# A two-layer expert behind a chunked mLSTM: the 64-row tail of w_in as pairs of 64-row products, the gates' weights summed in PSUM, and another order of work

## The chip, the cores and the metric

The kernel runs on one core of a Trainium2 chip. The time is device microseconds of one execution; before the change the median of three runs is 478.81 us (476.74 to 479.77). All times below are in microseconds unless a unit is given.

## The reference

Attention part, for every batch and head (B, H, S, D = 4, 8, 768, 40), step by step over S:

```python
m_new = np.maximum(f_gate[:, :, t] + m, i_gate[:, :, t])
f_stab = np.exp(f_gate[:, :, t] + m - m_new)
i_stab = np.exp(i_gate[:, :, t] - m_new)
C = f_stab[:, :, None, None] * C + i_stab[:, :, None, None] * np.einsum('bhd,bhe->bhde', vt, kt)
n = f_stab[:, :, None] * n + i_stab[:, :, None] * kt
h_tilde = np.einsum('bhde,bhe->bhd', C, qt)
denom = np.maximum(np.abs(np.einsum('bhd,bhd->bh', n, qt)[:, :, None]), 1.0)
y[:, :, t] = (1.0 / (1.0 + np.exp(-o_gate[:, :, t]))) * h_tilde / denom
```

Its y, heads side by side, is x [3072, 320]. Then the expert layer, in float32:

```python
h = x @ w_in                           # [320, 2048]
relu6 = np.clip(h + 3.0, 0.0, 6.0)
return ((h * relu6 / 6.0) @ w_out)     # [2048, 320]
```

## The kernel before, in words

**Tiling.** The 3072 tokens are eight units of 384 (three chunks of 128). For each unit the attention is made in two tasks of heads, chunk by chunk, and then x of this unit goes through the expert layer. Unit u+1's attention is made between the products of unit u.

**Gates** (`gates(c0, n)`, L415 to L504). The gates of all 32 (batch, head) rows are handled along the free axis, in four calls of 1, 1, 1 and 3 chunks (`GP`). On DVE: a scan gives the running maximum m (L439), two passes make the log forget factor (L445, L447), a second scan its running sum (L449), two subtractions the exponent of the input weight (L442, L460). PE then turns the results (L468, L469, L472) into the PSUM tile `pc`, DVE copies them out (L474, L477, L481), PE spreads each chunk's last column with the constant `last` (L495), DVE adds (L497), and ACT takes the exponentials wT, dec and eG (L483, L499, L501).

**Attention products** (`group`, L647). The tiles `xy` get batches of 16 small fp32 products each, 64 rows by 64 columns of the array: L669, L676, L685, L690. `fin` (L756) normalises, transposes to xa (L791) and splits x into xh (cast, L795) and xl (rest, L797).

**Expert weights.** w_in and w_out come as 64-bit words; `weight_slice` (L806) makes float32 of them in eight slices each, then splits w_in into fp32r parts: whi and wlo hold 256 of the 320 rows (as two tiles of 128 rows), and wtl the last 64 rows, high part in one half of the partitions and low part in the other. The tail's two casts (on ACT) and subtractions (L851, L852) are instructions of 64x128. `split_out` (L858) splits w_out into vh and vl.

**Expert products.** `mm1(u, f)` (L883) makes h of one feature block f (128 of 2048 features) for 384 tokens from eight products of 128 rows, 128 columns and 384 tokens (L895): six over the 256 rows, and two with wtl, which carry the tail's high and low weights in one product. `g = h * clip(h + 3, 0, 6) / 6` is an activation on ACT (L909) and a product with h on DVE (L911); then g is split into gh (L385) and gl (L919). `mm2(u, p)` (L924) multiplies two feature blocks with w_out: for each of three token tiles six products of 320 columns (L938 to L940). Unit 0 uses plain float32 there (L936). h has two PSUM buffers (`mm=2` in the plan's slots).

**Order.** All engines' instructions are put out in an order that a planner (`Plan`) works out when the kernel is built: every piece of work is a generator with a due time (worked out from constants such as T0, SPAN, AH and G0, plus an offset for its number from the table OFS), and the planner simulates the engines with fixed costs and takes what is ready and due first. `ENGINES` is a string of 30 letters: for each kind of elementwise work, which engines may do it. The scheduler then keeps this order. Until the expert layer opens (`open_moe`), PE is given filler products (`warm`, L403).

Of the kernel before, what the change touches and what calls it, by code (L numbers as in the profile page):

```python
# [49 lines left out]
T0H = -19.089  # L50
SP0 = 7.143
LST = 0.974
LVP = 0.547
LGW = 0.628
SPAN = 50.902
T0 = 57.141
AH = 8.377
GP = [1, 1, 1, 3]
G0 = 3.567
G1 = 5.981  # L60
AH1 = 33.544
# [65 lines left out]
class Plan:  # L127
# [119 lines left out]
    def run(self):  # L247
        self.settle()
        while self.jobs:
            best = {}  # L250
            for j in self.jobs:
# [14 lines left out]
                if j["hot"]:  # L266
                    start = max(self.free[e], 0.0)
                    if self.heat(start):
# [3 lines left out]
                        continue  # L272
                k = (late, start if late else 0.0, j["due"] + (j["req"][2] if len(j["req"]) > 2 and e != "q" else 0.0), j["n"])
# [55 lines left out]
def mlstm_moe_kernel(ctx: ExitStack, tc: tile.TileContext, ig, fg, qkd, natd, ond, w_in, w_out, ident_d, out):  # L329
# [31 lines left out]
    plan = Plan(dict(wm=1, xy=1, exy=1, z=1, es=1, eo=1, st=2, nat=2, gw=NGW, ht=2, on=1, x=2,  # L361
# [31 lines left out]
    def warm():  # L393
# [12 lines left out]
        f_s=[BR, S], i_s=[BR, S], m_s=[BR, S], lf=[BR, S], g_s=[BR, S], last=[128, 128], gTs=[128, NC, BH], cTs=[128, NC, BH], one=[BR, S // 2 + L], sel=[BR, 4, Q]).items()}  # L406
# [8 lines left out]
    def gates(c0, n):  # L415
        f_s, i_s, m_s, lf, g_s, last, gTs, cTs, one, sel = (GT[k] for k in ("f_s", "i_s", "m_s", "lf", "g_s", "last", "gTs", "cTs", "one", "sel"))
        if c0 == 0:
# [5 lines left out]
            nc.vector.memset(lf[:, 0:1], 0.0)  # L423
# [13 lines left out]
        hs = slice(c0, c0 + n)  # L437
        yield "d", ld(w)
        nc.vector.tensor_tensor_scan(m_s[:, a:z], f_s[:, a:z], i_s[:, a:z], m_s[:, a - 1 : a] if c0 else NEG, ALU.add, ALU.max)  # L439
        b, t = max(a, 1), plan.now["t"]  # L440
        e = yield psub(26, w)
        E(e).tensor_sub(i_s[:, a:z], i_s[:, a:z], m_s[:, a:z])  # L442
        ti, plan.now["t"] = plan.now["t"], t
        yield "d", ld(w)
        nc.vector.tensor_add(lf[:, b:z], f_s[:, b:z], m_s[:, b - 1 : z - 1])  # L445
        yield "d", ld(w)
        nc.vector.tensor_sub(lf[:, b:z], lf[:, b:z], m_s[:, b:z])  # L447
        yield "d", ld(2 * w)
        nc.vector.tensor_tensor_scan(g_s[:, a:z], one[:, :w], lf[:, a:z], 0.0, ALU.mult, ALU.add)  # L449
# [3 lines left out]
        t = plan.now["t"]  # L453
# [4 lines left out]
        plan.now["t"] = max(t, ti)  # L458
        yield "d", ld(w)
        nc.vector.tensor_sub(i_s[:, a:z], i_s[:, a:z], g_s[:, a:z])  # L460
        for c in cs:
            event(f"i_s{c}")
        yield "wait", "ident"
        gs = yield "get", "es"
        pc = bank(gs, [128, 3, n, BH], f"pc{c0}")
        yield "p", mat(6 * n, 64, 1, 32, 32)
        for c in cs:
            nc.tensor.transpose(pc[:, 0, c - c0, :], g_s[:BH, c * L : (c + 1) * L], ident[:BH, :BH])  # L468
            nc.tensor.transpose(pc[:, 1, c - c0, :], i_s[:BH, c * L : (c + 1) * L], ident[:BH, :BH])  # L469
        for s in range(2 * n):  # L470
            for h in range(2):
                nc.tensor.matmul(pc[h * Q : h * Q + Q, 2].rearrange("p n (c r) -> p (n c) r", c=2)[:, s], i_s[:BH, a + s * Q : a + s * Q + Q], ident[:BH, 16 * h : 16 * h + 16], start=True, stop=True)  # L472
        yield "d", cd(32 * n)
        nc.vector.tensor_copy(gTs[:, hs], pc[:, 0])  # L474
# [6 lines left out]
        nc.vector.tensor_copy(cTs[:, hs], pc[:, 1])  # L481
# [7 lines left out]
        go = yield "get", "eo"
        pl = bank(go, [128, 2, n, BH], f"pl{c0}")  # L490
        yield "p", mat(2, 32 * n, 2)
        nc.tensor.matmul(pl[:, 0], last, gTs[:, hs], start=True, stop=True)
        for c in range(2):
            for h in range(2):
                nc.tensor.matmul(pl[h * Q : h * Q + Q, 1].rearrange("p n (c r) -> p n c r", c=2)[:, :, c], last[:, c * Q : c * Q + Q], gTs[:, hs, 16 * h : 16 * h + 16], start=True, stop=True)  # L495
        yield "d", cd(32 * n)
        nc.vector.tensor_tensor(wT[:, hs], pl[:, 0], cTs[:, hs], ALU.add)  # L497
# [601 lines left out]
```

## Time and profile before

| | before |
|---|---|
| median of 3 runs | 478.81 us (476.74 to 479.77) |
| the profiled execution | 479.48 us, span 477.8 us |
| mean granted TensorE clock | 0.981 of full speed |
| instructions that count as work: PE, DVE, ACT, POOL | 5741, 811, 330, 259 |
| packets and bytes of DMA | 21245 packets, 47.66 MB |

The profile is that of one execution. "Busy" is the time in which an engine has an instruction of its own running; PE is TensorE's products, PEld its weight loads, which run beside them. A row of a group reads: line, engine, operation, output and inputs by their names, shapes, how often, then busy time and mean ns of one, then idle time of the engine just before and what ended it. A row of the timeline reads: start, duration, engine, line, operation, names, and in brackets the idle time before it. Products are pipelined: the next one starts before the last one's duration is over, so what a product costs is read from start to start. A window row reads: stretch, its length, busy time and instructions of PE, PEld, DVE, ACT and POOL, granted clock, share of the DMA engines' time, GB/s.

The page's list of groups also names idle time: POOL idles 158.1 us ahead of L919, 130.1 of them for gh, and ACT 186.1 us ahead of L909 for h.

### The profile page before, as it was taken

The page shows a single profiled execution, that of the slowest core. Times are in us where ns is not written, and L with a number is a line of the kernel's source. Part 1 is how long each engine was busy: PE and PEld are TensorE (multiplying, and loading weights), DVE is VectorE, ACT ScalarE, POOL GpSimd, SP SyncE. Part 2 cuts the span into 40 slices and gives each one's busy share as a digit, 9 for nine tenths or more (in the row PEclk, how much of TensorE's full clock was granted, in tenths as well). Part 3 has the DMA queues.
Part 4 walks back from the last instruction along what each step waited for, and adds up shares of the span by engine and source line. Part 5 has one row for each costly group of instructions (what it writes and reads, how often), then busy time and mean ns, then how long its engine had stood idle before and what let it go on. Part 6 is the DMA issues. An engine that isn't in the chain of part 4 may idle for free.

```text
span 477.8 us, 13585 instructions
## 1 busy us (share of the span) xinstructions
PE 464.4 (97%) x5741; PEld 435.8 (91%) x5741; DVE 307.4 (64%) x811; ACT 168.6 (35%) x330; POOL 185.9 (39%) x259
## 2 busy tenths in 40 slices
PE   8999889899999999999999999999999999999997
PEld 7898777777999999999999999999999999999996
DVE  5569799899878857576657466738554646334332
ACT  1234778895322422232324122322322221222112
POOL 3324331112565444445444353435453333333432
PEclk8599999999999999999999999999999999999999
DMA  7356678871152541435142151516041010001001
GB/s 238 96 163 232 173 253 242 240 269 49 43 150 57 137 140 53 115 79 150 45 122 70 50 143 37 115 44 177 16 117 43 2 43 3 1 1 42 1 1 41
DMA packets 21245, 47.66 MB, mean 100 GB/s; under 512 B 2360, under 2 KB 15416, under 8 KB 21184
## 3 DMA queue, kind: packets, MB, share of 16 engines
q1 hardware_dynamic: 21184, 46.79, 33.5%
q8 instruction: 45, 0.74, 0.7%
q14 instruction: 16, 0.13, 0.1%
HBM read 42.75 MB, written 4.03 MB: 98 GB/s over the span
## 4 chain that ended last, share of the span: by engine, by line
PE 86%; DVE 4%; ACT 4%; DMA 3%; issue 2%; SPq 0%; ACTq 0%; DVEq 0%
PE h L895 34%; PE acc L938 11%; PE acc L940 10%; PE acc L939 10%; PE pw L403 5%; PE xy L685 3%; PE xy L669 2%; PE xy L690 2%; PE acc L936 2%; PE xy L676 2%; PE xa L791 2%; DMA rawo<-in_w_out_dram 1%; DMA gw<-gsc 1%; ACT g L909 1%; DMA i_s<-in_ig_dram 1%
## 5 line engine op out<-in xcount | busy, mean ns | idle before, releaser
L919 POOL TENSOR_TENSOR gl<-g,gh 128x384 fp32r<-128x384 f32 x112 | 119.7, 1069 | 158.1 <-DVE gh L385 130.1
L911 DVE SCALAR_TENSOR_TENSOR g<-g,h 128x384 f32<-128x384 f32 x128 | 70.6, 552 | 128.3 <-ACT g L909 127.5
L909 ACT ACTIVATE g<-h,half 128x384 f32<-128x384 f32 x128 | 74.1, 579 | 204.8 <-PE h L895 186.1
L938 PE MATMUL acc<-vh,gh 128*128 128x320 f32 x336 | 104.3, 310 | 0.0
L940 PE MATMUL acc<-vh,gl 128*128 128x320 f32 x336 | 103.8, 309 | 0.0
L939 PE MATMUL acc<-vl,gh 128*128 128x320 f32 x336 | 103.5, 308 | 0.0
L895 PE MATMUL h<-xh,whi 128*128 128x384 f32 x256 | 93.7, 366 | 0.5 <-DVE g L911 0.5
L895 PE MATMUL h<-xl,whi 128*128 128x384 f32 x256 | 85.9, 336 | 0.0
L895 PE MATMUL h<-xh,wlo 128*128 128x384 f32 x256 | 85.9, 335 | 0.0
L938 PEld LDWEIGHTS acc<-vh,gh 128*128 128x128 f32 x336 | 63.0, 188 | 0.3
L940 PEld LDWEIGHTS acc<-vh,gl 128*128 128x128 f32 x336 | 63.0, 187 | 0.3 <-POOL gl L919 0.3
L939 PEld LDWEIGHTS acc<-vl,gh 128*128 128x128 f32 x336 | 63.0, 188 | 0.0
L729 POOL TENSOR_TENSOR C<-C,dec 128x84 f32<-128x84 f32 x77 | 30.8, 400 | 79.7 <-DVE C L731 56.2
L895 PEld LDWEIGHTS h<-xh,whi 128*128 128x128 f32 x256 | 48.1, 188 | 4.6 <-DVE g L911 2.0
L895 PEld LDWEIGHTS h<-xl,whi 128*128 128x128 f32 x256 | 48.3, 188 | 0.7
L895 PEld LDWEIGHTS h<-xh,wlo 128*128 128x128 f32 x256 | 48.1, 188 | 0.0
L385 DVE CAST gh<-g 128x384 fp32r<-128x384 f32 x112 | 42.1, 375 | 2.6
L895 PE MATMUL h<-xl,wtl 128*128 128x384 f32 x128 | 43.3, 338 | 0.0
L895 PE MATMUL h<-xh,wtl 128*128 128x384 f32 x128 | 43.0, 336 | 0.0
L573 POOL TENSOR_TENSOR nat<-nat,wT 128x168 f32<-128x168 f32 x48 | 27.6, 592 | 24.3 <-DMA nat<-in_nat_dram 17.5
L403 PE MATMUL pw<-ones 128*128 128x128 bf16 x397 | 30.9, 241 | 2.1 <-POOL ones L397 1.1
L936 PE MATMUL acc<-vr,g 128*128 128x320 f32 x96 | 28.0, 437 | 3.2 <-DVE vr L836 3.2
(107 smaller groups left out, 650.1 us busy)
## 6 DMA issues: line engine op xcount, KB each, us to landing
st<-in_qk_dram SPq DMA_DIRECT2D x28, 300.0 KB
nat<-in_nat_dram SPq DMA_DIRECT2D x16, 492.0 KB
gw<-gsc SPq DMA_DIRECT2D x28, 192.0 KB
rawi<-in_w_in_dram SPq DMA_DIRECT2D x8, 640.0 KB
rawo<-in_w_out_dram SPq DMA_DIRECT2D x8, 640.0 KB
nat<-in_nat_dram SPq DMA_DIRECT2D x16, 252.0 KB
on<-in_on_dram SPq DMA_DIRECT2D x8, 480.0 KB
out_dram<-ob SPq DMA_DIRECT2D x24, 160.0 KB
```

The source lines that it names most:

```text
L385: E(c).tensor_copy(dst, src)
L403: nc.tensor.matmul(pw[:, :WN], ones[:, :128], ones[:, :WN], start=True, stop=True)
L573: E(e).tensor_tensor(v, v, heads(wT[:, c], bq)[:, :, :, None].broadcast_to([128, 2, 2, E2]), ALU.mult)
L729: nc.gpsimd.tensor_tensor(Cn[:R], cur[:R], dc[:, :, None].broadcast_to([R, 2, E2]), ALU.mult)
L895: nc.tensor.matmul(hp, w, x, start=n == 0, stop=n == len(seq) - 1)
L909: nc.scalar.activation(g, hp, AF.Relu, bias=half, scale=1.0 / 6.0)
L911: nc.vector.scalar_tensor_tensor(g, g, 1.0, hp, ALU.min, ALU.mult)
L919: E(e).tensor_sub(gl, g, gh.bitcast(F32))
L936: nc.tensor.matmul(acc, gh[:, ts_], VR[p].bitcast(F32)[:, f % 2, :], start=f == 0, stop=f == NF - 1)
L938: nc.tensor.matmul(acc, gh[:, ts_], VH[f // 4][:, f % 4, :], start=f == 0, stop=False)
L939: nc.tensor.matmul(acc, gh[:, ts_], VL[p][:, f % 2, :], start=False, stop=False)
L940: nc.tensor.matmul(acc, gl[:, ts_], VH[f // 4][:, f % 4, :], start=False, stop=f == NF - 1)
```

## The change

1. **The tail.** whi and wlo become [128, 8, 640]: 512 columns as before and 128 for the tail, where the even block's 64 rows lie in partitions 0 to 63 and the odd block's in 64 to 127. One cast and one subtraction of 128x640 for each slice take the place of casts and subtractions of three pieces. mm1 of an even block f makes its six full products (L901) and then six products of 64 rows (L909), alternately rows 0 to 63 into h_f and rows 64 to 127 into h_{f+1}; mm1 of f+1 makes only its six full products. The h_{f+1} buffer is taken ahead of the half products.
2. **Gates.** Two calls of 2 and 4 chunks. The first subtraction is gone: the forget factor's scan works in place on f_s with an addition only at the points where the sum restarts (every 64 steps, L447), and one subtraction makes g_s. For wT and dec DVE makes a product with the identity (`diag`, L474) and PE sums everything in PSUM, in one trip, through products that accumulate (L480, L482, L484). `lf`, `last`, `gTs`, `cTs` and the PSUM slot `eo` are gone; `es` has two buffers. wT, dec and eG are announced apart; `state` waits for dec, `back` for eG.
3. **Order of work.** New constants and a new table OFS, `ENGINES` of new letters and a second string ENG2 that holds from 150 us of the planner's time (TSW). By this gh's casts go mostly from DVE to ACT (96 of 112), gl's subtractions from POOL to DVE (all 112, L933 instead of L919), the cast of whi from ACT to DVE and vh's from DVE to ACT, 24 of 48 POOL operations of `weigh` to ACT. Fillers are 371 instead of 397. SP loads st ahead of nat and w_out's first slice ahead of w_in's; the gates go out in two pieces instead of four. The end of the program has another order of mm1 and mm2 (below).

```diff
-    whi = wts.tile([128, 2, FF], F32R, name="whi")
-    wlo = wts.tile([128, 2, FF], F32R, name="wlo")
-    wtl = wts.tile([128, FF], F32R, name="wtl")
+    whi = wts.tile([128, WS, WC], F32R, name="whi")
+    wlo = wts.tile([128, WS, WC], F32R, name="wlo")
...
-GP = [1, 1, 1, 3]
+GP = [2, 4]
...
-ENGINES = 'yawzzapdyzyxypydxyzdxxapwyzydx'
+ENGINES = 'dpwaaxpdapaaydydxydadxwwdazydy'
+ENG2 = 'xapdydzdpwdpzyzyxawwzypwyyzyza'
+TSW = 150.0
...
+    def bank_mm(u, f):
+        if (u, f) not in HT:
+            HT[u, f] = P["mm"].tile([128, NT], F32, tag=f"mm{HP[u, f][1]}", name=f"h{u}_{f}")
+        return HT[u, f]
...
-        got = yield "get", "mm"
-        hp = P["mm"].tile([128, NT], F32, tag=f"mm{got[1]}", name=f"h{u}_{f}")
-        fs = slice(f * 128, (f + 1) * 128)
-        seq = [(whi[:, 0, fs], xh[:, 0, :]), (whi[:, 0, fs], xl[:, 0, :]), (wlo[:, 0, fs], xh[:, 0, :]),
-               (whi[:, 1, fs], xh[:, 1, :]), (whi[:, 1, fs], xl[:, 1, :]), (wlo[:, 1, fs], xh[:, 1, :]),
-               (wtl[:, fs], xh[:, 2, :]), (wtl[:, fs], xl[:, 2, :])]
-        yield "p", mat(8, NT)
-        for n, (w, x) in enumerate(seq):
-            nc.tensor.matmul(hp, w, x, start=n == 0, stop=n == len(seq) - 1)
+        i, r = divmod(f, 2)
+        if r == 0:
+            HP[u, f] = yield "get", "mm"
+        hp = bank_mm(u, f)
+        yield "p", mat(6, NT)
+        for k in range(2):
+            wc = slice(k * 256 + r * 128, k * 256 + r * 128 + 128)
+            for n, (w, x) in enumerate(((whi, xh), (whi, xl), (wlo, xh))):
+                nc.tensor.matmul(hp, w[:, i, wc], x[:, k], start=r == 0 and k == 0 and n == 0, stop=r == 1 and k == 1 and n == 2)
+        if r == 0:
+            HP[u, f + 1] = yield "get", "mm"
+            h2 = bank_mm(u, f + 1)
+            yield "p", mat(3, NT)
+            for n, (w, x) in enumerate(((whi, xh), (whi, xl), (wlo, xh))):
+                for a, dst in enumerate((hp, h2)):
+                    rs = slice(a * Q, a * Q + Q)
+                    nc.tensor.matmul(dst, w[rs, i, 512:640], x[rs, 2], start=a == 1 and n == 0, stop=a == 0 and n == 2)
...
+        nc.vector.tensor_add(f_s[:, b:z:Q], f_s[:, b:z:Q], m_s[:, b - 1 : z - 1 : Q])
...
+        nc.vector.tensor_tensor_scan(f_s[:, a:z], one[:, :w], f_s[:, a:z], 0.0, ALU.mult, ALU.add)
...
+        nc.vector.tensor_tensor(gd, g_s[:BH, a + Q - 1 : z : Q].rearrange("p (n c) -> p n c", c=2)[:, :, :, None].broadcast_to([BH, n, 2, BH]), ident[:BH, None, None, :BH].broadcast_to([BH, n, 2, BH]), ALU.mult)
...
+        nc.tensor.matmul(pc[:, 0], one[:BH, 1:2].broadcast_to([BH, 128]), gd[:, :, 1], start=True, stop=False)
+        for c in cs:
+            nc.tensor.matmul(pc[:, 0, c - c0], i_s[:BH, c * L : (c + 1) * L], ident[:BH, :BH], start=False, stop=c == c0 + n - 1)
...
+        nc.scalar.activation(wT[:, hs], pc[:, 0], AF.Exp)
...
-        nc.vector.tensor_copy(gTs[:, hs], pc[:, 0])
...
-        nc.vector.tensor_tensor(wT[:, hs], pl[:, 0], cTs[:, hs], ALU.add)
```

How the instructions move stands in the programs' orders. First PE in the last unit, at blocks 14 and 15; before (h_14's last product is followed by h_15's first, then mm2 of blocks 12 and 13):

```order
L895 MATMUL h_14_6610<-xh_5686,wlo 128x384
L895 MATMUL h_14_6610<-xh_5686,wtl 128x384
L895 MATMUL h_14_6610<-xl_5687,wtl 128x384
L895 MATMUL h_15_6627<-xh_5686,whi 128x384
...
L895 MATMUL h_15_6627<-xl_5687,wtl 128x384
L938 MATMUL acc_0_6336<-vh_2049,gh_12_6578 128x320
```

and now, from h_14's last full product on:

```order
L901 MATMUL h_14_6714<-xh_5842,wlo 128x384
L909 MATMUL h_14_6714<-xh_5842,whi 128x384
L909 MATMUL h_15_6745<-xh_5842,whi 128x384
L909 MATMUL h_14_6714<-xl_5843,whi 128x384
...
L952 MATMUL acc_0_6421<-vh_1969,gh_12_6699 128x320
...
L901 MATMUL h_15_6745<-xh_5842,wlo 128x384
L952 MATMUL acc_0_6421<-vh_1969,gh_14_6753 128x320
```

The half products write to both h_14 and h_15, mm2 of blocks 12 and 13 has moved ahead of h_15's full products, and behind these stands at once mm2 of blocks 14 and 15.

Second, DVE in the first call of the gates and the next; before:

```order
L439 SCALAR_TENSOR_TENSOR m_s<-f_s,i_s 36x128
L445 TENSOR_TENSOR lf<-f_s,m_s 36x127
L447 TENSOR_TENSOR lf<-lf,m_s 36x127
L449 SCALAR_TENSOR_TENSOR g_s<-one,lf 36x128
L439 SCALAR_TENSOR_TENSOR m_s<-f_s,m_s,i_s 36x128
L460 TENSOR_TENSOR i_s<-i_s,g_s 36x128
...
L474 COPY gTs<-pc_208 128x32
...
L481 COPY cTs<-pc_208 128x32
...
L497 TENSOR_TENSOR wT<-pl_247,cTs 128x32
```

and now (all of the gates' DVE work but the second cT):

```order
L444 SCALAR_TENSOR_TENSOR m_s<-f_s,i_s 36x256
L447 TENSOR_TENSOR f_s<-f_s,m_s 36x3
L450 COPY f_s<-i_s 36x1
L452 SCALAR_TENSOR_TENSOR f_s<-one,f_s 36x256
L455 TENSOR_TENSOR g_s<-f_s,m_s 36x256
L466 TENSOR_TENSOR i_s<-i_s,f_s 36x256
L444 SCALAR_TENSOR_TENSOR m_s<-f_s,m_s,i_s 36x512
L474 TENSOR_TENSOR diag<-g_s,ident 32x128
...
L503 COPY cT<-pc_233 128x64
L474 TENSOR_TENSOR diag<-g_s,ident 32x256
```

Both calls come one behind the other, without an instruction between that waits for a second trip of PE.

Third, DVE at the end of the program; before, and now:

```order
L911 SCALAR_TENSOR_TENSOR g_14_6623<-g_14_6623,h_14_6610 128x384
L385 CAST gh_14_6624<-g_14_6623 128x384
L911 SCALAR_TENSOR_TENSOR g_15_6639<-g_15_6639,h_15_6627 128x384
L385 CAST gh_15_6640<-g_15_6639 128x384
L955 COPY ob_1_6680<-acc_1_6349 128x320
```

```order
L925 SCALAR_TENSOR_TENSOR g_14_6752<-g_14_6752,h_14_6714 128x384
L933 TENSOR_TENSOR gl_14_6754<-g_14_6752,gh_14_6753 128x384
L925 SCALAR_TENSOR_TENSOR g_15_6783<-g_15_6783,h_15_6745 128x384
L933 TENSOR_TENSOR gl_15_6785<-g_15_6783,gh_15_6784 128x384
L969 COPY ob_1_6803<-acc_1_6447 128x320
```

Where gh was cast, gl is now subtracted, behind a cast that has moved to ACT.

On SP, the loads of a task are now st ahead of nat. On all engines, counts of instructions go from 4532 to 4594 on PE, from 813 to 770 on DVE, from 332 to 562 on ACT and from 264 to 124 on POOL.

More of the change, by code (lines that the diff above doesn't have):

```diff
@@ L405, in mlstm_moe_kernel @@
     GT = {k: early["ea"].tile(sh, F32, name=k) for k, sh in dict(
-        f_s=[BR, S], i_s=[BR, S], m_s=[BR, S], lf=[BR, S], g_s=[BR, S], last=[128, 128], gTs=[128, NC, BH], cTs=[128, NC, BH], one=[BR, S // 2 + L], sel=[BR, 4, Q]).items()}
+        f_s=[BR, S], i_s=[BR, S], m_s=[BR, S], g_s=[BR, S], diag=[BH, NC, 2, BH], one=[BR, S // 2 + L], sel=[BR, 4, Q]).items()}
     maskb = early["ea"].tile([128, Q], BF16, name="maskb")
@@ L415, in gates @@
     def gates(c0, n):
-        f_s, i_s, m_s, lf, g_s, last, gTs, cTs, one, sel = (GT[k] for k in ("f_s", "i_s", "m_s", "lf", "g_s", "last", "gTs", "cTs", "one", "sel"))
+        f_s, i_s, m_s, g_s, diag, one, sel = (GT[k] for k in ("f_s", "i_s", "m_s", "g_s", "diag", "one", "sel"))
         if c0 == 0:
@@ L437, in gates @@
         hs = slice(c0, c0 + n)
-        yield "d", ld(w)
[L439 to L449, printed above, removed]
+        yield "d", ld(2 * w)
+        nc.vector.tensor_tensor_scan(m_s[:, a:z], f_s[:, a:z], i_s[:, a:z], m_s[:, a - 1 : a] if c0 else NEG, ALU.add, ALU.max)
+        b = max(a, Q)
+        yield "d", Lock(0.07)
+        nc.vector.tensor_add(f_s[:, b:z:Q], f_s[:, b:z:Q], m_s[:, b - 1 : z - 1 : Q])
+        if c0 == 0:
+            yield "d", Lock(0.07)
+            nc.vector.tensor_copy(f_s[:, 0:1], i_s[:, 0:1])
+        yield "d", ld(2 * w)
+        nc.vector.tensor_tensor_scan(f_s[:, a:z], one[:, :w], f_s[:, a:z], 0.0, ALU.mult, ALU.add)
+        t = plan.now["t"]
+        yield "d", ld(w)
+        nc.vector.tensor_sub(g_s[:, a:z], f_s[:, a:z], m_s[:, a:z])
         for c in cs:
@@ L457, in gates @@
             event(f"gsc{c}")
-        plan.now["t"] = max(t, ti)
-        yield "d", ld(w)
-        nc.vector.tensor_sub(i_s[:, a:z], i_s[:, a:z], g_s[:, a:z])
+        plan.now["t"] = t
+        e = yield psub(26, w, cg(w) + 0.25)
+        E(e).tensor_sub(i_s[:, a:z], i_s[:, a:z], f_s[:, a:z])
+        plan.now["t"] = max(plan.now["t"], tg)
         for c in cs:
@@ new lines, in gates @@
+        for h in range(2):
+            nc.tensor.matmul(pc[h * Q : h * Q + Q, 1].rearrange("p n (c r) -> p n c r", c=2), one[:BH, 1:2].broadcast_to([BH, Q]), gd[:, :, :, 16 * h : 16 * h + 16], start=True, stop=True)
+        t = plan.now["t"]
+        yield "a", ca(32 * n)
+        nc.scalar.activation(wT[:, hs], pc[:, 0], AF.Exp)
+        for c in cs:
+            event(f"wT{c}")
+        yield "a", ca(32 * n)
+        nc.scalar.activation(dec[:, hs].rearrange("p n c r -> p n (c r)"), pc[:, 1], AF.Exp)
@@ L470, in gates @@
+        for c in cs:
+            event(f"dec{c}")
+        te, plan.now["t"] = plan.now["t"], t
+        yield "p", mat(1, 64, 1, 32, 32).times(8 * n)
+        for c in cs:
+            nc.tensor.transpose(pc[:, 2, c - c0], g_s[:BH, c * L : (c + 1) * L], ident[:BH, :BH])
         for s in range(2 * n):
             for h in range(2):
-                nc.tensor.matmul(pc[h * Q : h * Q + Q, 2].rearrange("p n (c r) -> p (n c) r", c=2)[:, s], i_s[:BH, a + s * Q : a + s * Q + Q], ident[:BH, 16 * h : 16 * h + 16], start=True, stop=True)
@@ L489, in gates @@
[L489 to L497, printed above, removed]
@@ L656, in group @@
         cost.w = dur * 1200.0
+        cost.cx = 1.6
         yield "p", cost
@@ L840, in weight_slice @@
         if kind == "i":
[L841 to L854 removed]
+            e = yield pcast(24, WC)
+            cast(e, whi[:, i], w)
+            e = yield psub(7, WC)
+            E(e).tensor_sub(wlo[:, i], w, whi[:, i].bitcast(F32))
         put(*gy)
```

141 lines of the change are left out of this document (63 added, 78 removed).

## The prediction

> **What bounds the kernel now.** I read the totals and the chain that ended last first, then windows cut where the character of the work changes (first product of the expert layer at 56.8 us, one unit later, the attention's end), then the instruction timeline at the places that the edit touches.
>
> ```profile
> PE 464.4 (97%) x5741; PEld 435.8 (91%) x5741; DVE 307.4 (64%) x811; ACT 168.6 (35%) x330; POOL 185.9 (39%) x259
> PE 86%; DVE 4%; ACT 4%; DMA 3%; issue 2%; SPq 0%; ACTq 0%; DVEq 0%
> ```
>
> ```profile
> 0.00:15.00 15.00, 13.61 (x139) 11.81 (x140) 7.98 (x30) 2.96 (x8) 6.05 (x20) 0.79 0.67 220
> 15.00:30.00 15.00, 15.00 (x271) 13.80 (x270) 8.03 (x28) 2.54 (x9) 5.12 (x10) 0.64 0.44 138
> 30.00:57.00 27.00, 23.65 (x619) 21.54 (x617) 22.34 (x76) 16.55 (x35) 8.65 (x14) 1.00 0.57 175
> 57.00:113.00 56.00, 51.21 (x578) 42.45 (x578) 53.08 (x129) 47.28 (x83) 12.24 (x18) 1.00 0.76 237
> 113.00:165.00 52.00, 52.00 (x698) 47.95 (x697) 44.41 (x111) 15.60 (x31) 25.95 (x32) 1.00 0.33 89
> 165.00:405.00 240.00, 239.57 (x3016) 230.41 (x3015) 146.41 (x392) 66.89 (x133) 102.86 (x142) 1.00 0.29 78
> ```
>
> The columns are the stretch, its length, then busy time of PE, PEld, DVE, ACT and POOL. From 113 to 405 us PE is busy 291.57 of 292 us: there only a change of PE's own time counts, and DVE, ACT and POOL have room (146.41 of 240 for DVE). From 57 to 113 PE idles 4.8 us and DVE is full (53.08 of 56): its casts and subtractions feed PE. Before 57 us PE's busy share is padding by L403, and what counts is how soon the chain of gates, attention and x allows the first product; DVE idles 14 of the first 30 us and is nearly full after.
>
> **Part 1, the half products.** Each pair of feature blocks had 16 products of 384 columns and gets 15 product times, if two 64-row products really run side by side. The price of a product and that of leaving the 128x128 mode stand in one stretch, where an attention visit interrupts block after block:
>
> ```profile
> 242.43 0.34 PE L895 MATMUL h<-xh,wtl 128*128 128x384 f32 x1
> 242.60 0.34 PE L895 MATMUL h<-xl,wtl 128*128 128x384 f32 x1
> 242.87 0.44 PE L685 MATMUL xy<-C,st 40*64 40x42 f32 x16
> 243.12 0.42 PE L690 MATMUL xy<-nat,gw 64*64 64x42 f32 x16
> 243.36 0.44 PE L669 MATMUL xy<-st 40*64 40x64 f32 x16
> 243.62 0.40 PE L676 MATMUL xy<-nat 64*64 64x42 f32 x16
> 243.94 0.44 PE L895 MATMUL h<-xh,whi 128*128 128x384 f32 x1
> 244.23 0.33 PE L895 MATMUL h<-xl,whi 128*128 128x384 f32 x1
> 244.40 0.33 PE L895 MATMUL h<-xh,wlo 128*128 128x384 f32 x1
> ```
>
> One product is 0.173 us (242.43 to 242.60). Saved: 64 pairs x 0.173 = 11.1 us. The four groups of 16 small products take 0.25 each, 16 at a time, so small tiles do run together. But from the last full product to the first small one it is 0.27 instead of 0.17, and the first full product after the visit takes 0.29 instead of 0.17. From 242.60 to 244.23 are 1.63 us; two products (0.35) and four groups (1.00) leave 0.28 us for going out of the mode and back.
>
> The new order has 64 visits to the half mode, one per pair; 14 of their 128 boundaries are shared with an attention visit, and attention visits go from 53 to 54. Of the shared ones each saves half a visit's price, so the price counts 64 - 7 = 57 times, plus 0.28: net cost = 57p + 0.3 - 11.1. No row shows a 64-row, 128-column visit, so p is bounded. Only the rows change here, at the gates' transposes:
>
> ```profile
> 26.52 0.83 PE L403 MATMUL pw<-ones 128*128 128x128 bf16 x12
> 27.29 0.24 PE L468 MATMUL pc<-ident,g_s 32*128 32x32 f32 x1
> 27.37 0.22 PE L469 MATMUL pc<-ident,i_s 32*128 32x32 f32 x1
> 27.44 0.22 PE L468 MATMUL pc<-ident,g_s 32*128 32x32 f32 x1
> ```
>
> Twelve fillers in 0.83, the last itself 0.22, are 0.056 apart, which puts the last at 27.14; the first 32-row transpose follows 0.15 later (+0.09) and the second 0.08 after it, the next 0.07 (+0.01 to 0.02): a low end of 0.11. The high end is a visit that pays the delay at the start (0.10) and the slow first product (0.12) on both sides: 0.44. I take 0.28, the attention visit whole: it leaves the same products, returns to the same products and costs them both ways, while the low end has neither their weights nor the way back in it. That gives 57 x 0.28 = 16.0, + 0.3 - 11.1 = +5.2 us. Eight of the 64 visits lie in the stretch from 57 to 113 us where PE idles 4.8 us, so 7/8 counts: **+4.5 us**. At 0.11 it is -4.0, at 0.44 +12.5, at nothing -9.4.
>
> The Trainium skill ("TensorEngine Tiling (Array Packing)", Tiling Modes) says "Mode switching requires drain: Changing tiling mode (not just tile) drains the TensorE"; it gives no time, and the trace agrees that a switch costs, with the 0.28 above. By that rule alone, whatever the drain, part 1 gains less than 11.1. Against it, "TensorE: Matmul & The Clock Gate" (Part 3, Measured speedup vs the span model) has row tiles spaced by about 4 ns, 3.07 times for four; by that page alone the whole 11.1 us would be had.
>
> **PSUM.** h_{f+1}'s buffer is now taken at the half products, six products earlier. How late a buffer comes free stands in the last unit:
>
> ```profile
> 421.71 0.34 PE L895 MATMUL h<-xl,wtl 128*128 128x384 f32 x1
> ...
> 422.14 0.58 ACT L909 ACTIVATE g<-h,half 128x384 f32<-128x384 f32 x1 [3.44 <-PE h L895]
> ...
> 422.75 0.55 DVE L911 SCALAR_TENSOR_TENSOR g<-g,h 128x384 f32<-128x384 f32 x1 [3.07 <-ACT g L909]
> ...
> 423.36 0.44 PE L895 MATMUL h<-xh,whi 128*128 128x384 f32 x1
> ```
>
> From the last product into a buffer to its next use are 1.65 us (L909, then L911). Eight products of another block lie between before, 1.39 from the same start plus one, so the wait is 0.09. After, where a block f odd is followed at once by f+1 and its half products, only seven product times (1.21) lie between: 0.44 of waiting. In the new order six places have that, most of them in the last unit; before four have the small wait. 6 x 0.44 - 4 x 0.09 = 2.3, and the drain of the mode (0.10 each) passes inside the wait: **+1.6**; bounds 0 (the wait covers the entry wholly) and 2.3.
>
> **The end.** Before, mm2 of blocks 12 and 13 (18 products) stands between the last mm1 and its own mm2. Now mm1 15 directly precedes mm2 of blocks 14 and 15, and gl is made on DVE instead of POOL, gh on ACT instead of DVE:
>
> ```profile
> 469.20 0.58 ACT L909 ACTIVATE g<-h,half 128x384 f32<-128x384 f32 x1 [1.00 <-PE h L895]
> ...
> 469.81 0.55 DVE L911 SCALAR_TENSOR_TENSOR g<-g,h 128x384 f32<-128x384 f32 x1 [0.56 <-ACT g L909]
> ...
> 470.47 0.36 DVE L385 CAST gh<-g 128x384 fp32r<-128x384 f32 x1
> ```
>
> ```profile
> L795 ACT CAST xh<-xa 128x384 fp32r<-128x384 f32 x21 | 9.9, 473 | 7.8 <-PE xa L791 7.8
> L797 DVE TENSOR_TENSOR xl<-xa,xh 128x384 fp32r<-128x384 f32 x21 | 11.6, 552 | 5.4 <-ACT xh L795 5.4
> ```
>
> The L795 and L797 rows are the same two operations on the same shape and engines. After the last product: 0.43 until L909 begins, 0.61 to L911, 0.6 to the cast, 0.47 for it: gh_15 is there 2.1 us after. Three products of block 14 come first (320 columns each, 0.145 by the 384 columns' 0.173, so 0.44), after one product time, so PE waits about 1.5, and for gl_15 about 0.3 more, since later groups need it: **+1.8** (bounds 1.3 and 2.3).
>
> **Part 2, the gates and the head.** A g needs an x, an x needs gates, w_in needs its split; all of it goes through DVE:
>
> ```profile
> L449 DVE TENSOR_TENSOR_SCAN g_s<-one,lf 36x128 f32<-36x128 f32 (+1 forms) x4 | 2.4, 588 | 0.1
> L460 DVE TENSOR_TENSOR i_s<-i_s,g_s 36x128 f32<-36x128 f32 (+1 forms) x4 | 1.7, 430 | 0.0
> L447 DVE TENSOR_TENSOR lf<-lf,m_s 36x128 f32<-36x128 f32 (+2 forms) x4 | 1.7, 418 | 0.1
> L445 DVE TENSOR_TENSOR lf<-f_s,m_s 36x128 f32<-36x128 f32 (+2 forms) x4 | 1.6, 408 | 0.0
> L474 DVE COPY gTs<-pc 128x32 f32<-128x32 f32 (+1 forms) x4 | 0.8, 208 | 4.1 <-PE pc L472 4.1
> L497 DVE TENSOR_TENSOR wT<-pl,cTs 128x32 f32<-128x32 f32 (+1 forms) x4 | 0.8, 208 | 4.7 <-PE pl L495 4.7
> L481 DVE COPY cTs<-pc 128x32 f32<-128x32 f32 (+1 forms) x4 | 0.8, 190 | 0.0
> L851 DVE TENSOR_TENSOR wtl<-yi,wtl 64x128 fp32r<-64x128 f32 x8 | 2.3, 286 | 0.2
> L852 DVE TENSOR_TENSOR wtl<-yi,wtl 64x128 fp32r<-64x128 f32 x8 | 3.6, 445 | 0.2
> ```
>
> L445's full pass becomes an add of 3 and 8 columns (-1.3), the passes of L447 and L460 are made twice instead of four times (-0.6 each), the scans too (-0.2): -2.7. L474, L481 and L497 go (-2.4), with a constant and two trips of cT (-0.5). Three slices are split ahead of the first g; their six tail subtractions go, 3 x (0.286 + 0.445) = -2.2. The diagonal product adds 0.5. Two casts of w_in, wider wlo, one more added slice less two shifts and a little attention work that the new order puts ahead add about 2.3 (estimate from rows of 0.3 to 0.9). DVE has about 5 us less to do before the first g, and the two waits for PE of 4.1 and 4.7 us become one shorter round. I take **-5 us**: since PE has hardly a gap later, an earlier first product is an earlier end, one for one. Ends: -8, if this also ends PE's stall here, which isn't tied to one of these operations:
>
> ```profile
> 54.59 0.43 PE L676 MATMUL xy<-nat 64*64 64x42 f32 x13 [2.30 <-issue]
> ```
>
> and -3, if the stretch from 57 to 113, where DVE is the bound, gives part of it back: up to the first block of unit 1 DVE has 2 us more to do in the new order, much of it vl made ahead of need.
>
> **The rest** I cost at nothing: casts and subtractions moved between DVE, ACT and POOL lie, from 165 us on, beside a PE that is always busy, with DVE at 61% (146.41 of 240). gl comes to DVE, 0.55 us a block, and gh (0.36) mostly leaves it, so DVE has 0.2 us more a block there. Without the cover it would be rival C. Loads are reordered on SP; from 165 us on DMA is at 0.29 of its time.
>
> **Sum:** +4.5 + 1.6 + 1.8 - 5 = +2.9 against the profiled execution's 479.48 us (span 477.8), so 482.4; that execution is 0.7 above the median of 478.81, so 481.7. I give **481.5 us**. 1% is 4.8 us, about what a measurement of this kernel can tell from no change.
>
> **Rivals.** With the other terms as above, the end moves by 0.875 x (57p - 10.8) - 1.6: faster by over 1% below p = 0.13, slower by over 1% above p = 0.32.
>
> A. *Row tiles hardly switch.* If changing only rows costs what the transposes show, 0.11, the sum is -4.0 + 3.4 - 5 = -5.6, **474 us**; if nothing, -9.4 + 3.4 - 5 = -11, 468, and 465 with the head's best end. For it: the row of the transposes. Against it: the 0.12 on the first full product after the attention visit, which waits for full-width weights however few rows were used before.
>
> B. *Every entry and exit shows its weights (slower).* The half products also load weights, into rows that the full products still use. If both sides pay 0.22, p = 0.44: +12.5 + 3.4, and only -3 from the head: **491 us**. It decides from p = 0.32. For it: PEld is at 91%, so there is little room to load ahead. Against: half weights are half as many rows.
>
> C. *DVE becomes the bound in unit 1 (slower).* gl moves to DVE there while gh still stays: 15 blocks x 0.55 = 8.3 us on 44.41 of 52 is 52.7, with 2 us of backlog from unit 0: about +3 beyond the forecast, **485 us**. Against it: the attention work there can be put off.
>
> D. *Half products run one after another.* Three slots more per pair, 64 x 0.52 = 33 us: **515 us**. The 16 small products in 0.25 us speak against it.
>
> **How the numbers follow.** Forecast 0.42 (faster 0.06, same 0.28, slower 0.08; its own range 475 to 487 by the head's ends and p from 0.20 to 0.34). A 0.33 (faster 0.27, same 0.06). B 0.16 (slower 0.15, same 0.01). C 0.06 (slower 0.05, same 0.01). D 0.03 (slower). Together faster 0.33, same 0.36, slower 0.31. The range runs from A's best end, 465, to B, 491; outside are D and half of the extremes of A and B.
>
> **What would show it.** In the new profile, the time from the last full product to the first half product, and of the first full one after, gives p: 0.10 and 0.12 more than 0.17 fit the forecast; 0.17 on both sides is A. Pairs of half products 0.17 apart, two starting together, show D wrong. First expert product near 52 us shows the head right. A DVE share near 1 from 113 to 165 with PE idle shows C. A gap of 1.5 to 2 us before the last mm2 shows the end's term. I am wrong if part 1 is cheap, or if the head gains much more than the DVE work it loses.

## The result, and the profile after

The changed kernel takes 490.26 us (median of four runs, 489.71 to 494.74) against 478.35 for the kernel before beside it: a ratio of 1.027, 95% interval 1.020 to 1.034. It is slower by 11.9 us. The forecast was 481.5 (no change likeliest); the measured time lies at the upper end of the range, at the time that rival B gave (491).

The totals and the chain that ended last, after:

```profile
PE 476.6 (98%) x5821; PEld 421.0 (86%) x5821; DVE 301.6 (62%) x768; ACT 241.6 (50%) x560; POOL 50.2 (10%) x119
PE 90%; DMA 4%; DVE 2%; issue 2%; ACT 1%; SPq 0%; DVEq 0%; ACTq 0%
```

PE is still the bound, and more so (90% of the chain, 86% before): its busy time has risen by 12.2 us, with fewer product times to do. The windows of before, again:

```profile
15.00:30.00 15.00, 15.00 (x245) 13.78 (x244) 5.92 (x22) 2.06 (x7) 2.66 (x7) 0.64 0.53 167
30.00:57.00 27.00, 24.70 (x601) 22.08 (x601) 22.08 (x72) 11.52 (x22) 7.92 (x17) 0.94 0.57 160
57.00:113.00 56.00, 55.28 (x605) 42.34 (x604) 53.08 (x125) 46.35 (x72) 7.59 (x15) 1.00 0.77 235
113.00:165.00 52.00, 50.39 (x589) 44.54 (x588) 41.50 (x111) 18.72 (x38) 8.49 (x18) 0.97 0.33 89
165.00:405.00 240.00, 239.10 (x3096) 215.57 (x3096) 139.85 (x366) 129.03 (x354) 18.71 (x45) 1.00 0.28 78
```

PE now fills the first unit too (55.28 of 56, where 51.21 stood), so part of what the half products cost there can have come out of idle time. From 165 to 405 it is as full as before. DVE has not become the bound from 113 to 165 (41.50 of 52); PE's one long pause there, 1.61 us ahead of L678, comes in the middle of a group of attention products, and the profile names nothing that ended it.

One visit to the half mode, and the first and the last expert product of the program:

```profile
53.92 0.44 PE L901 MATMUL h<-xh,whi 128*128 128x384 f32 x1
...
300.06 0.34 PE L901 MATMUL h<-xl,whi 128*128 128x384 f32 x1
300.24 0.34 PE L901 MATMUL h<-xh,wlo 128*128 128x384 f32 x1
300.51 0.44 PE L909 MATMUL h<-xh,whi 64*128 64x384 f32 x2
300.79 0.33 PE L909 MATMUL h<-xl,whi 64*128 64x384 f32 x2
300.96 0.33 PE L909 MATMUL h<-xh,wlo 64*128 64x384 f32 x2
301.22 0.42 PE L952 MATMUL acc<-vh,gh 128*128 128x320 f32 x1
301.47 0.31 PE L953 MATMUL acc<-vl,gh 128*128 128x320 f32 x1
301.62 0.31 PE L954 MATMUL acc<-vh,gl 128*128 128x320 f32 x1
...
484.56 0.30 PE L954 MATMUL acc<-vh,gl 128*128 128x320 f32 x1
```

The x2 are the pairs: two half products begin together, so they do run side by side. But four steps are too long: 0.27 to the first pair and 0.28 to the second instead of 0.17, 0.26 from the last pair to the first full product instead of 0.17, and 0.25 to the next instead of 0.147. These are 0.095 + 0.107 + 0.09 + 0.107 = 0.40 us for a visit, and so it is in all 32 visits of this profile that share no boundary and meet no other wait (0.396 to 0.406). Why the second step is long, the weight loads of the same visit show:

```profile
300.07 0.19 PEld L901 LDWEIGHTS h<-xh,wlo 128*128 128x128 f32 x1
300.50 0.19 PEld L909 LDWEIGHTS h<-xh,whi 64*128 64x128 f32 x2 [0.25 <-issue]
300.61 0.19 PEld L909 LDWEIGHTS h<-xl,whi 64*128 64x128 f32 x2
300.79 0.19 PEld L909 LDWEIGHTS h<-xh,wlo 64*128 64x128 f32 x2
301.22 0.19 PEld L952 LDWEIGHTS acc<-vh,gh 128*128 128x128 f32 x1 [0.24 <-issue]
301.33 0.19 PEld L953 LDWEIGHTS acc<-vl,gh 128*128 128x128 f32 x1
```

In the steady run a load begins with the product ahead of it, one product early. At each change of mode the first load begins only with its own product (300.50, 301.22, after 0.25 of nothing), and the second 0.11 later: the lead is lost and built up again, on the way in and on the way out. The Trainium skill ("TensorEngine Tiling (Array Packing)", Key Properties) says that a change of tiling mode drains the engine, and gives no time for it. The 0.25 without a weight load at both changes fits that; the ends of products are modelled, so the drain itself can't be read from the profile.

From the first to the last product are 430.65 us (53.92 to 484.56), before 417.25 (56.81 to 474.06): +13.4, of which an earlier start gives 2.9 back; the spans differ by 10.3.

### The profile page after: what moved, and what is told of

Read it like the earlier page. It is cut to its first block, busy times and chain, and to the rows that moved or that the text cites. A ratio compares the mean times of both kernels' runs of the same rounds, so it can differ in the third digit from the quotient of the medians.

```text
span 488.1 us, 13701 instructions
## 1 busy us (share of the span) xinstructions
PE 476.6 (98%) x5821; PEld 421.0 (86%) x5821; DVE 301.6 (62%) x768; ACT 241.6 (50%) x560; POOL 50.2 (10%) x119
## 4 chain that ended last, share of the span: by engine, by line
PE 90%; DMA 4%; DVE 2%; issue 2%; ACT 1%; SPq 0%; DVEq 0%; ACTq 0%
PE h L901 27%; PE acc L952 12%; PE acc L954 10%; PE acc L953 10%; PE h L909 9%; PE pw L409 5%; PE acc L950 3%; PE xy L694 3%; PE xy L678 3%; PE xy L699 2%; PE xy L685 2%; PE xa L800 2%; DMA rawo<-in_w_out_dram 2%; DMA rawi<-in_w_in_dram 1%; DMA i_s<-in_ig_dram 1%
## 5 line engine op out<-in xcount | busy, mean ns | idle before, releaser
L952 PE MATMUL acc<-vh,gh 128*128 128x320 f32 x336 | 108.3, 322 | 1.4 <-ACT gh L388 1.4
L901 PE MATMUL h<-xh,whi 128*128 128x384 f32 x256 | 93.7, 366 | 0.0
L901 PE MATMUL h<-xh,wlo 128*128 128x384 f32 x256 | 86.3, 337 | 0.5 <-DVE wlo L852 0.4
L901 PE MATMUL h<-xl,whi 128*128 128x384 f32 x256 | 85.9, 336 | 0.0
L933 DVE TENSOR_TENSOR gl<-g,gh 128x384 fp32r<-128x384 f32 x112 | 62.2, 557 | 23.9 <-ACT gh L388 21.9
L388 ACT CAST gh<-g 128x384 fp32r<-128x384 f32 x96 | 48.9, 510 | 32.4 <-DVE g L925 32.4
L738 POOL TENSOR_TENSOR C<-C,dec 128x84 f32<-128x84 f32 x79 | 32.6, 416 | 285.2 <-DVE C L740 201.7
L901 PEld LDWEIGHTS h<-xh,whi 128*128 128x128 f32 x256 | 48.0, 188 | 5.3 <-issue 3.2
L901 PEld LDWEIGHTS h<-xh,wlo 128*128 128x128 f32 x256 | 48.2, 188 | 1.1 <-DVE wlo L852 1.1
L901 PEld LDWEIGHTS h<-xl,whi 128*128 128x128 f32 x256 | 48.2, 188 | 0.6
L409 PE MATMUL pw<-ones 128*128 128x128 bf16 x371 | 29.1, 244 | 3.3 <-issue 2.3
L909 PE MATMUL h<-xh,whi 64*128 64x384 f32 x128 | 31.5, 441 | 0.2
L409 PEld LDWEIGHTS <-ones 128*128 128x128 bf16 x371 | 25.8, 110 | 4.7 <-issue 2.7
L909 PEld LDWEIGHTS h<-xh,whi 64*128 64x128 f32 x128 | 13.5, 183 | 16.6 <-issue 14.2
```

The source lines that it names most:

```text
L388: nc.scalar.copy(dst, src)
L409: nc.tensor.matmul(pw[:, :WN], ones[:, :128], ones[:, :WN], start=True, stop=True)
L738: nc.gpsimd.tensor_tensor(Cn[:R], cur[:R], dc[:, :, None].broadcast_to([R, 2, E2]), ALU.mult)
L901: nc.tensor.matmul(hp, w[:, i, wc], x[:, k], start=r == 0 and k == 0 and n == 0, stop=r == 1 and k == 1 and n == 2)
L909: nc.tensor.matmul(dst, w[rs, i, 512:640], x[rs, 2], start=a == 1 and n == 0, stop=a == 0 and n == 2)
L933: E(e).tensor_sub(gl, g, gh.bitcast(F32))
```

## The experiments

Three theories stood at the start: the visits' own price (about 0.40 each), the price of the prediction (0.28) with the rest lost in the new order of work, and the order of work alone.

**No visits.** The three pairs become three full products; the order on all engines stays that of the change.

```diff
-                for a, dst in enumerate((hp, h2)):
-                    rs = slice(a * Q, a * Q + Q)
-                    nc.tensor.matmul(dst, w[rs, i, 512:640], x[rs, 2], start=a == 1 and n == 0, stop=a == 0 and n == 2)
+                nc.tensor.matmul(hp if n else h2, w[:, i, 512:640], x[:, 2], start=n == 0, stop=n == 2)
```

> Leaves out: the tail's two blocks are not kept apart. Each pair of feature blocks gets three full 128-row products (one into the odd block's h, two into the even one's) in place of the three pairs of 64-row products; all else, and the order on every engine, is that of the change. Theory 1 (the visits to the 64-row mode cost about 0.40 us each: in the changed kernel's trace 0.095 at the entry, 0.107 ahead of the second pair, 0.09 at the exit, 0.107 ahead of the second full product; 14 shared boundaries save some 2.8 us): 64 x 0.395 - 2.8 = 22.5 us less, about 468 us. Theory 2 (the attention visit's 0.28, with the rest of the loss in the order of work): 57 x 0.28 = 16 us less, 474 us. Theory 3 (the order of work alone): 490 us.

470.6 us, ratio to before 0.981 (0.974 to 0.988): 19.7 less than the change, by the same number of product times. The order alone is out. Theory 1 is nearest. From the first to the last product its profile has 409.53 us, 21.1 less than the change, and PE idles 1.1 us more in them. So most of the 2.8 that are missing to 22.5 are a later first product (below) and waits that the visits had covered. In the last unit the same wait for a PSUM buffer that lies inside a visit in the change now stands bare:

```profile
417.33 0.34 PE L901 MATMUL h<-xh,wlo 128*128 128x384 f32 x1
417.95 0.44 PE L907 MATMUL h<-xh,whi 128*128 128x384 f32 x1 [0.28 <-DVE g L923]
418.23 0.34 PE L907 MATMUL h<-xl,whi 128*128 128x384 f32 x1
418.40 0.34 PE L907 MATMUL h<-xh,wlo 128*128 128x384 f32 x1
```

It also shows that the 0.28 to the second product can follow a break without a change of mode.

**Twice the visits.** The even block's sixth full product is put between the first pair and the second.

Here `one(m)` issues the m-th of the six full products.

```diff
+        for m in range(6 - (r == 0)):
+            one(m)
...
             for n, (w, x) in enumerate(((whi, xh), (whi, xl), (wlo, xh))):
                 for a, dst in enumerate((hp, h2)):
...
+                if n == 0:
+                    one(5)
```

> The change with twice the visits: the even block's sixth full product stands between the first and the second pair of half products, so each visit becomes two; products and order otherwise the same. Theory 1: 64 more visits at 0.395: 25 us more, 515 us. Theory 2: 64 x 0.28 = 18 more, 508 us. Theory 3: 490 us.

518.22 us, ratio 1.081 (1.073 to 1.089): 28.0 more than the change for 64 more visits, 0.44 each, well over theory 2. From the first to the last product it is 457.20 against 430.65, 0.41 a visit, as theory 1 had it; the rest is a later first product. The stretch shows the price in its purest form:

```profile
415.16 0.34 PE L903 MATMUL h<-xl,whi 128*128 128x384 f32 x1
415.43 0.44 PE L914 MATMUL h<-xh,whi 64*128 64x384 f32 x2
415.80 0.44 PE L903 MATMUL h<-xh,wlo 128*128 128x384 f32 x1
416.17 0.44 PE L914 MATMUL h<-xl,whi 64*128 64x384 f32 x2
416.46 0.33 PE L914 MATMUL h<-xh,wlo 64*128 64x384 f32 x2
416.72 0.41 PE L959 MATMUL acc<-vh,gh 128*128 128x320 f32 x1
```

Where modes alternate product by product, each step is 0.37 instead of 0.173: **0.20 us for a change of mode**, in either direction.

**Part 1 taken back, the order kept.** The tail stacked as before, four full products in place of the six half ones.

```diff
+            for a, dst in enumerate((hp, h2)):
+                tl = wtl[:, (f + a) * 128 : (f + a) * 128 + 128]
+                nc.tensor.matmul(dst, tl, xh[:, 2], start=a == 1, stop=False)
+                nc.tensor.matmul(dst, tl, xl[:, 2], start=False, stop=a == 0)
```

> The change with its part 1 taken back and its order kept: w_in's tail stacked as before, four full products (two for each block) where the six half products stood. Theory 1: 22.5 us less for the visits and 64 x 0.173 = 11.1 more for the products: about 479 us, no different from before. Theory 2: 16 less and 11.1 more, 485 us. Theory 3: 490 + 11 = 501 us.

484.9 us, ratio 1.011 (1.003 to 1.020), where theory 1 gave 479 and theory 2 gave 485. Taken alone it would speak for theory 2, but more than the visits differs in it: the tail's subtractions and casts are back on DVE in an order that was planned without them, and PE waits for wlo, which it never did in the kernel before:

```profile
L908 PE MATMUL h<-xh,wlo 128*128 128x384 f32 x256 | 86.6, 338 | 3.0 <-DVE wlo L859 3.0
```

Against the run without visits, which has the same order, the waits account for it: from the first to the last product are 422.89 us, 13.4 more than 409.53, and the 64 products more (11.1) and 2.6 us more of idle time in PE make 13.7. So the nearness to theory 2 is luck, and the two runs above, which change the visits alone, decide.

**Part 1 alone, part 2 alone, both, on the planner's constants of before.** The first has `mm1` and the split of w_in as in the diff of the change, the second `gates` and its events with two calls (offsets renumbered), the third both; the third differs from the change in the order of work and the engines of the casts only. The first two edits, cut to a line each:

```diff
-        yield "p", mat(8, NT)
+        yield "p", mat(6, NT)
```

```diff
-GP = [1, 1, 1, 3]
+GP = [2, 4]
```

> The kernel before with part 1 alone (the half products and the wide whi and wlo); gates, constants and table of offsets are those of before. It has 64 visits to the 64-row mode, 19 boundaries shared with attention visits, and the same end as the change (the last mm1 directly ahead of its own mm2). Theory 1 (0.395 a visit): 25.3 - 3.8 for the shared ones - 11.1 = +10.4, a little hidden where PE idles in the first unit, +2 at the end and +1.5 for PSUM: about 491 us. Theory 2 (0.28): 64 x 0.28 - 2.7 - 11.1 = +4.1, and the same 3.5: 486 us. Theory 3 (the half products are worth their 11 us and the new table is what costs): 467 us.

491.25 us, ratio 1.028 (1.024 to 1.031): +13.4 for part 1 alone, as theory 1 had it, without anything of the new table. In the first unit PE is busy 54.83 of 56 us there, before 51.21.

> The kernel before with part 2 alone (gates in two calls, sums in PSUM); mm1, constants and offsets are those of before, the offsets renumbered for the two calls that are gone. If DVE's work ahead of the first g sets the first expert product, the first product comes 3 to 5 us earlier than at 56.8 us, and the time is 474 to 476 us. Rival (the loads and the split of w_in set it, so that the gates only end earlier): first product at 56 to 57 us, 478 us.

475.1 us, ratio 0.996 (0.994 to 0.998): 2.8 us less by the medians, 2.0 by the ratio, and so a little faster than both kernels of this case. The time is the one that was expected; whether it came by the expected way isn't shown. The execution that was profiled is the slowest of ten (478.44 us). In it the first product is no earlier:

```profile
56.78 0.69 PE L897 MATMUL h<-xh,whi 128*128 128x384 f32 x1
```

```profile
30.00:57.00 27.00, 17.57 (x384) 14.79 (x377) 25.23 (x73) 18.50 (x38) 9.66 (x14) 0.64 0.57 172
57.00:113.00 56.00, 55.16 (x586) 46.02 (x587) 51.01 (x122) 45.62 (x77) 19.44 (x22) 0.96 0.67 216
```

By these windows DVE does more of its work ahead of 57 us (25.23 of 27, before 22.34), and PE then idles 0.8 us in the first unit, not 4.8; from the first to the last product it is 415.93 us, 1.3 less than before. The 3.3 us by which the median lies under this execution stand in no profile.

> The kernel before with parts 1 and 2, on before's constants and offsets; it differs from the change in the order of work and in the engines of the casts alone. If the parts add up, it is the time with part 1 alone plus the gain or loss of part 2. If the new table of the change is worth something for these parts, this kernel is slower than the change's 490 us; if the new table costs time, it is faster.

487.64 us, ratio 1.022 (1.018 to 1.025). The parts about add up (+13.4 - 2.8 = +10.6; measured +9.8). It is 2.6 us under the change, with intervals of the ratios that overlap. In the profiles the difference lies ahead of the first product, which comes here at

```profile
51.45 0.45 PE L897 MATMUL h<-xh,whi 128*128 128x384 f32 x1
```

against 53.92 in the change; from there to the last product it is 430.8 us here and 430.65 there. So the new table and the moved casts bring nothing after the head. In the head, 2.5 us are no more than what one order varies by. Three runs have the change's instructions, in its order, up to the first expert product: the last block's mm1 moved (below), no visits, and twice the visits. In their profiles it begins at

```profile
54.18 0.44 PE L901 MATMUL h<-xh,whi 128*128 128x384 f32 x1
...
55.51 0.44 PE L901 MATMUL h<-xh,whi 128*128 128x384 f32 x1
...
56.55 0.44 PE L903 MATMUL h<-xh,whi 128*128 128x384 f32 x1
```

and in the change's own at 53.92. So it isn't shown that the new table costs anything in the head.

**The end.** The last block's mm1 goes ahead of most of mm2 of blocks 12 and 13, in the change.

```diff
-            plan.add(T0 + SPAN * u + SPAN * f / NF - MV, mm1(u, f), pre + [f"wi{f//2}", f"fin{2*u+1}_2", "mo"], 0)
+            plan.add(T0 + SPAN * u + SPAN * f / NF - MV - 8.0 * (u == NU - 1 and f == NF - 1), mm1(u, f), pre + [f"wi{f//2}", f"fin{2*u+1}_2", "mo"], 0)
```

> The change with the last feature block's mm1 ahead of mm2 of blocks 12 and 13 for two of their three token tiles; nothing else moves. If the gap of 1.6 us and the slow products after it (2.0 us in all ahead of the last mm2) are a wait for gh_15 and gl_15 that other products can cover: 2.0 us less, 488.3 us. Rival (another wait takes its place, such as the last copies out): no change, 490 us.

487.84 us, ratio 1.018 (1.011 to 1.025), 2.4 less than the change; the intervals overlap, but all four executions (486.75 to 489.03) lie under all of the change's. The change's end was

```profile
479.91 0.33 PE L901 MATMUL h<-xh,wlo 128*128 128x384 f32 x1
480.08 0.31 PE L952 MATMUL acc<-vh,gh 128*128 128x320 f32 x1
480.23 0.31 PE L953 MATMUL acc<-vl,gh 128*128 128x320 f32 x1
480.37 0.31 PE L954 MATMUL acc<-vh,gl 128*128 128x320 f32 x1
482.11 0.42 PE L952 MATMUL acc<-vh,gh 128*128 128x320 f32 x1 [1.43 <-ACT gh L388]
482.37 0.30 PE L953 MATMUL acc<-vl,gh 128*128 128x320 f32 x1
482.70 0.41 PE L954 MATMUL acc<-vh,gl 128*128 128x320 f32 x1
```

and now twelve products of older blocks stand between; of the wait only 0.13 is left, ahead of gl_15:

```profile
479.24 0.31 PE L952 MATMUL acc<-vh,gh 128*128 128x320 f32 x1
479.38 0.31 PE L953 MATMUL acc<-vl,gh 128*128 128x320 f32 x1
479.66 0.41 PE L954 MATMUL acc<-vh,gl 128*128 128x320 f32 x1
```

**Is it the clock that holds the head back?** Part 2 alone had 171 fillers and a granted clock of 0.64 from 30 to 57 us. Two kernels raise `RATE` alone, by which the planner puts in more fillers.

The second takes 3520.727.

```diff
-RATE = 1841.626
+RATE = 2700
```

> The kernel before with part 2 alone, and RATE of 2700 instead of 1841.626, by which the planner puts in 377 fillers instead of 171 and orders other work a little differently. With part 2 alone the granted clock was 0.64 from 30 to 57 us (1.00 before), and the first expert product came at 56.8 us in the profile, as before. If the low clock holds the head back, a clock near 1 there brings the first product 3 to 5 us earlier, as DVE's work would allow, and the time to 471 to 473 us. Rival: DVE, busy 25.2 of these 27 us, is the bound, and the clock changes nothing: 475 us.

> As the run with RATE 2700, with 3520.727, the change's value: 408 fillers. The same two outcomes: 471 to 473 us if the clock holds the head back, 475 us if DVE does.

482.77 us (ratio 1.008, 1.005 to 1.011) and 481.02 us (1.006, 1.002 to 1.010): both theories fail. The clock rose to 0.81 and 0.97 there, and in the profiles (of executions of 482.85 and 482.29 us) the first product came at 63.2 and 58.7 us. The window of the second:

```profile
30.00:57.00 27.00, 23.52 (x604) 21.76 (x604) 21.90 (x70) 14.32 (x31) 8.66 (x17) 0.97 0.48 137
```

DVE has less done by 57 us there (21.90, with part 2 alone 25.23) at the higher clock. But that isn't the cause either: in the first of the two DVE is busy 26.01 of these 27 us, and its first product is the latest of all. The planner's order of all engines shifts with the fillers, so the two runs show that a higher clock bought with fillers doesn't pay here; they don't part the clock from the order. What sets the first product of part 2 alone stays open, all the more as the 56.8 us are from its slowest execution.

## Why the prediction was wrong, point by point

**The price of a visit** is the step that failed: "I take 0.28, the attention visit whole". It is 0.40. By the prediction's own formula, 57 x 0.40 + 0.3 - 11.1 = +12.0 instead of +5.2. It was chosen because the attention visit "leaves the same products, returns to the same products and costs them both ways". That holds for the way out of the full mode and for the return, but not for the inside. By starts, the attention visit has 0.10 on the way in, 0.07 to the first full product behind it (0.32, where its groups are 0.25 apart) and 0.12 to the second; the half visit has 0.095, 0.09 and 0.107 at these places. But its second pair waits 0.107 more for its weights, and the attention visit has next to nothing there: its small products begin in fours, 0.079 apart at first and then 0.058, so 0.02 late. Why the small products are spared was not tested. The signs that the prediction named, 0.10 and 0.12, were met almost exactly; the step inside the visit was not among them. The low end from the gates' transposes (0.11) left out the return.

**Rival B** was right in mechanism and time: every entry and exit shows its weights, with 0.20 on each side where it had 0.22, and 491 us against 490.26. Its point of decision (0.32) was passed. The reason that the prediction held against it, "half weights are half as many rows", is refuted by the rows above, where a half load takes 0.19 as a full one does. Rival A rested on the transposes' row, which has no way back in it. D fell with the pairs that start together, C with DVE at 41.50 of 52.

**Eight visits in idle time** (the factor 7/8): right in kind. With part 1 alone PE's busy time in the first unit goes from 51.21 to 54.83 of 56. In the change (55.28) part 2 has a share in it, since part 2 alone has 55.16 without a visit.

**PSUM**, +1.6: six places with 0.44, less the drain. The profile has five in the last two units, of 0.34 behind the entry:

```profile
422.84 0.34 PE L901 MATMUL h<-xh,wlo 128*128 128x384 f32 x1
423.11 0.78 PE L909 MATMUL h<-xh,whi 64*128 64x384 f32 x2
423.46 0.61 PE L909 MATMUL h<-xl,whi 64*128 64x384 f32 x2
423.74 0.51 PE L909 MATMUL h<-xh,wlo 64*128 64x384 f32 x2
```

Here the pair isn't together: its first product begins at 423.11, its second (which opens h_{f+1}) as late as the next group's, at 423.46. 5 x 0.34 = 1.7: right in size. Two more, of 0.57 and 0.54, lie in the first unit.

**The end**, +1.8: 2.0 by the profile (480.08 to 484.56 are 4.48 us, 17 product steps of 0.146 make 2.49), 2.4 by the run that removes it. Right.

**The head**, -5: the first product came 2.9 us earlier in the change's profile, and 0.3 to 2.6 earlier in the three others with the same instructions ahead of it. So the term fell short, and a single profile doesn't fix its size. DVE's work ahead of the first product was counted about right (33.88 us, before 38.16), but the amount of it isn't what sets that product: with both parts on the old table it came 5.8 us earlier than with part 1 alone (51.45 and 57.28) behind nearly the same work on DVE (37.74 and 38.38 us). "One for one" is the second step that failed.

**The sum** with the measured sizes: 25.6 for 64 visits at 0.40, less 2.8 for 14 shared boundaries at 0.20 (the one at 169.6 us saves 0.21), 0.3 more for an attention visit, less 11.1 saved: +12.0. The end +2.0, PSUM +1.7 less before's small waits, 0.4. PE's idle time from 57 to 405 us, by the windows, 5.2 before and 3.2 after: -2.0. The head -2.9. That is +10.4, and the spans differ by 10.3. Against the forecast's +2.9, the visits less the idle time (+10.0 where +4.5 stood) make 5.5 of the difference and the head 2.1.

## What to carry to other kernels

A saving in products is set against the changes of mode that it needs: here 0.173 us saved for each pair of blocks, and two changes at 0.20 paid. The price of going out of a mode and back is read from start to start over the first two products on each side, for the products that will stand there: the visit of small products gave 0.28 where the half products paid 0.40. An operand that is made on another engine after the last product of a block wants other products between: without them the end of this program took 2 us more. And how early a first product comes is compared over several executions: here it moved by 2.6 us without a change in the instructions ahead of it.

## What the runs showed of the hardware

A change of tile rows between 128 and 64, with products of 384 columns in fp32r, costs 0.20 us each way: about 0.09 until the first product of the new mode and 0.107 ahead of the second, whose weights are loaded late. The second part also came without a change of mode, behind a wait for PSUM (0.28 to the second product). Loading the weights of 64 rows takes as long as of 128 (0.19). Two products on different rows begin 0.003 to 0.004 us apart.
